# Attention and gated feed-forward on one core: head 0's bias rows built in place, V's first piece issued sooner, and the prologue's transposes and scores in another order

## The chip, the cores and the metric

One core of one Trainium2 chip. The metric is the device time of one execution in microseconds (us); before the change the median of 11 runs is 376.83 us (375.98 to 380.3). Engines are named as in the profile: PE is TensorE (PEld its weight loads), DVE is VectorE, ACT is ScalarE, POOL is GpSimd, SP is SyncE, which here only issues DMAs.

## The reference

Eight batches, eight heads, 576 positions, head size 64. Each head attends causally with a decay bias that comes from a running sum of `max(s, 0)`; the result, as 4608 rows of 512, goes through a gated feed-forward with 1536 hidden columns.

```python
scores = scale * np.matmul(q, k.transpose(0, 1, 3, 2))
cum = np.cumsum(np.maximum(s, 0.0), axis=-1)
bias = -(cum[:, :, :, None] - cum[:, :, None, :])
scores = np.where(causal, -1000000000.0, scores + np.minimum(bias, 0.0))
attn = np.exp(scores - np.max(scores, axis=-1, keepdims=True))
attn = attn / (np.sum(attn, axis=-1, keepdims=True) + 1e-09)
attn_out = np.matmul(attn, v)
# x: attn_out as (B * S, H * D)
g = x @ w_gate
out = (g * (1.0 / (1.0 + np.exp(-g))) * (x @ w_val)) @ w_out
```

## The kernel before, in words

**Bias as matrix rows.** A score is a product over 128 partitions. For an even row r of heads, 64 partitions hold q or k; the other 64 hold four bias rows and zeros. The running sum, scaled by 8 (`c8`), is split into a bf16 high part and a bf16 remainder. Two of the four rows multiply these parts on k's side by ones on q's side, the other two multiply q's parts by minus ones on k's side. All rows of all 64 heads stand in `HL` (partition = head, then four rows, then the q side and the k side). `aug` (L178) copies them by DMA, one head at a time, into `KQ[hb % 2][r]`, where `hb` is a group of four heads. A head is `hh` in its group, `r, e = divmod(hh, 2)`: r picks the tile, e its half of the columns. So heads 0 and 1 share `KQ[0][0]`, heads 2 and 3 share `KQ[0][1]`, heads 4 to 7 the two tiles of `KQ[1]`.

**The prologue.** SP loads s, then k and q of hb 0 in halves (row r = 0, then row 1). ACT, DVE and POOL fill the constant and zero parts of the tiles (L197 to L224; `pads` and `init_vt` are memsets on POOL). POOL then issues k's and q's loads of hb 1. DVE makes `HL` in a chain (L226 to L232): scale s, scan, high part, remainder, copy. k and q are cast to bf16 (`cast_half` for hb 0, `cast_one` for whole groups), transposed by PE into PSUM banks (`row_half` L886 for hb 0, `half_batch` L892 for hb 1) and copied out into `KQ` by `pe_out` (L305), which runs as L314 on ACT and as L316 on DVE. `keep_warm` issues products of the identity that nothing reads.

**The order by hand.** From L906 on, the calls stand in the order in which each engine gets its instructions; every engine and every queue works in that order[...]. `scores(h)` is four calls of `score_piece` (L338): a mask product (L353) for the pieces on the diagonal, the score products (L359), one exponential on ACT (L369). `values` is the product with V (L396) and the division on DVE (L412, L413). V is loaded in five pieces by POOL (`load_v` L151) and cast into `VT` by `cast_v` (L162), four pieces on POOL and one on DVE. `x_pe` transposes the attention's output, and `begin` (L630) starts the feed-forward. From then on `attn_items` and `ffn_items` are interleaved.

**Banks.** PSUM has eight banks. `take()` (L120) gives the one that was released longest ago, so the order of the calls also decides which earlier reader a product waits for. hb 1's transposed k and q hold four banks until their eight outputs are copied.

Of the kernel before, what the change touches and what calls it, by code (L numbers as in the profile page):

```python
# [12 lines left out]
FP32 = mybir.dt.float32  # L13
BF16 = mybir.dt.bfloat16
AF = mybir.ActivationFunctionType
ALU = mybir.AluOpType
# [3 lines left out]
def kernel(  # L20
# [11 lines left out]
    nc = tc.nc  # L32
    PSUM = bass.MemoryType.PSUM

    B, H, S, D = q.shape
# [42 lines left out]
    )  # L78

    NPE = 5  # L80
    XB = 2
    KS = {i: dram.tile([NR * S, 128], BF16, name=f"ks{i}") for i in range(NPE, NHB)}
    XS = {
# [11 lines left out]
    VT = [const.tile([128, NCH, H, D + 1], BF16, name=f"vt{i}") for i in range(2)]  # L95
    ident = const.tile([128, 128], BF16)
    one_s = const.tile([128, 1], FP32)
    HL = const.tile([BH, 4, 2, S], BF16)
    XR = 3 * TT
    XT = const.tile([128, 4, XR], BF16)  # L100
    warm = const.tile([128, 1], FP32)
    WS = const.tile([128, NFT // 2, 3, DM // 2], BF16)
    first_sbuf = ExitStack()
    first = first_sbuf.enter_context(tc.tile_pool(name="first", bufs=1))
    s_sb = first.tile([BH, S], FP32)
    c8 = first.tile([BH, S], FP32)
    PTP = {0: first, "bufs": 7}
    lower = first.tile([128, 512], BF16)

    with tc.manual_schedule():  # L110
# [76 lines left out]

        nc.sync.dma_start(s_sb, s.rearrange("b h n -> (b h) n"))
        def init_vt(i):
            nc.gpsimd.memset(VT[i][:, :, :, D : D + 1], 1.0)  # L190
            nc.gpsimd.memset(VT[i][64:128, 4, :, 0:D], 0.0)

        for r in range(NR):
            load_one(0, "k", (r, r + 1))
# [5 lines left out]
        nc.vector.memset(HL[:, 0:2, 0, :].bitcast(FP32), ONES2)  # L200
        nc.vector.memset(HL[:, 2:4, 1, :].bitcast(FP32), NEGS2)
        make_identity(nc, ident)
        nc.gpsimd.memset(lower, 0.0)
        nc.gpsimd.affine_select(
# [1 line left out]
            compare_op=ALU.is_ge, fill=nc.gpsimd.to_reg(MASKED), base=0, channel_multiplier=-1,  # L206
        )

        def pads(i):
            for r in range(2):  # L210
                nc.gpsimd.memset(KQ[i][r][64 * r : 64 * r + 64, :, NR * S :], 0.0)
# [8 lines left out]
        nc.vector.memset(aug_rows(1, 0), 0.0)  # L220
        for nm in ("k", "q"):
            load_one(1, nm, eng=nc.gpsimd)
        init_vt(0)
        pads(1)  # L224

        nc.vector.tensor_scalar(s_sb, s_sb, 0.0, 8.0, ALU.max, ALU.mult)  # L226
        nc.vector.tensor_tensor_scan(
            c8, one_s[0:BH, 0:1].to_broadcast([BH, S]), s_sb, 0.0, ALU.mult, ALU.add
        )
        nc.vector.tensor_copy(HL[:, 0, 1, :], c8)  # L230
        nc.vector.tensor_sub(HL[:, 1, 1, :], c8, HL[:, 0, 1, :])
        nc.vector.tensor_copy(HL[:, 2:4, 0, :], HL[:, 0:2, 1, :])  # L232

        SP4 = [nc.sync] * 4
        GP4 = [nc.gpsimd] * 4
# [69 lines left out]
        def pe_out(hb, name, g, r, eng):  # L305
            j0, j1 = JG[g]
            kq = SRC[name][1]
            dst = KQ[hb % 2][r][64 * r : 64 * r + 64, kq, 0 : NR * S].rearrange(
                "a (x j) -> a x j", j=J
            )[:, :, j0:j1]  # L310
            tp = tps[name, g]
            srcp = tp[0][64 * r : 64 * r + 64].rearrange("a j x -> a x j")
            if eng is nc.scalar:
                nc.scalar.copy(dst, srcp)  # L314
            else:
                eng.tensor_copy(dst, srcp)  # L316
            tp[2] -= 1
            if tp[2] == 0:
                give(tp[1])
# [577 lines left out]
        def scores(h):  # L897
            for ci in range(4):
                score_piece(h, ci)
# [23 lines left out]
        cast_one(1, "q", nc.vector)  # L923
        for c in range(3):
# [141 lines left out]
```

## Time and profile before

| | before |
|---|---|
| median of 11 runs | 376.83 us (375.98 to 380.3) |
| the profiled execution, its own time | 376.11 us |
| its span, first to last instruction | 374.4 us |
| mean granted TensorE clock | 0.998 |
| head 0's first score product | 11.02 us |
| first exponential | 11.45 us |
| first feed-forward product (L630) | 26.27 us |

The span is the time between the first and the last instruction of the profiled execution; the rest of its time lies around it. A row of the trace names start and duration in us, engine, line, operation, output and input with shapes, the number of instructions that were merged, and in square brackets the idle time before them with what ended it. All durations below come from this one execution. Busy times of TensorE are modelled and overlap, so one looks at the starts of its products.

### The profile page before, as it was taken

Reading aid. Unit: us, or ns where it says so; the run is one execution under the profiler, and the core shown is the slowest. Engines: PE = TensorE matmul, PEld = TensorE weight load, DVE = VectorE, ACT = ScalarE, POOL = GpSimd, SP = SyncE. Lnnn points to the kernel's source line nnn. Section 1 sums busy time; section 2 is a strip of 40 time slices with the busy share of each in tenths; the row PEclk is TensorE's granted clock in tenths of the full one; section 3 lists DMA queues with packets and bytes.
Section 4 is the critical chain, followed back from the end, with each engine's and each line's share of the span. In section 5 each row is a group of like instructions: output and inputs, shape, how many; then the busy total and the mean of one; then the engine's idle time right before and its main releaser. Section 6 shows DMA issues by size and latency. Waiting matters only on the chain.

```text
span 374.4 us, 8759 instructions
## 1 busy us (share of the span) xinstructions
PE 362.1 (97%) x3259; PEld 231.0 (62%) x3300; DVE 289.9 (77%) x578; ACT 240.3 (64%) x471; POOL 212.3 (57%) x325
## 2 busy tenths in 40 slices
PE   7799999999999999999999999999999999999995
PEld 6575556555555556855685559655865585476464
DVE  8968776468984899589967997699858867975984
ACT  8877776688876878588757875686566523323321
POOL 8983655856465647494649564955675516315320
PEclk9999999999999999999999999999999999999999
DMA  7899999899599997796769674995142103002003
GB/s 243 192 269 261 213 273 260 215 340 208 173 175 274 264 259 205 178 290 204 204 160 265 181 176 160 259 193 134 40 119 62 35 20 127 2 0 94 21 0 114
DMA packets 97146, 64.23 MB, mean 172 GB/s; under 512 B 77232, under 2 KB 82736, under 8 KB 97104
## 3 DMA queue, kind: packets, MB, share of 16 engines
q1 hardware_dynamic: 84976, 41.46, 46.3%
q0 software_dynamic: 12128, 22.21, 22.8%
q8 instruction: 26, 0.43, 0.5%
q14 instruction: 16, 0.13, 0.1%
HBM read 37.90 MB, written 19.86 MB: 154 GB/s over the span
## 4 chain that ended last, share of the span: by engine, by line
PE 90%; DVE 3%; ACT 3%; issue 1%; DMA 1%; POOL 1%; SPq 0%; DVEq 0%; ACTq 0%
PE bank L630 46%; PE bank L736 17%; PE bank L359 11%; PE bank L396 8%; PE bank L687 5%; ACT pt L369 2%; DVE kq L316 1%; DMA rawq<-in_q_dram 1%; PE bank L446 1%; ACT kq L314 1%; DVE pp L653 1%; POOL vt L168 1%; DVE ht L664 1%; PE bank L353 1%; PE bank L287 1%
## 5 line engine op out<-in xcount | busy, mean ns | idle before, releaser
L369 ACT ACTIVATE pt<-bank 128x512 bf16<-128x512 f32 (+1 forms) x256 | 120.3, 510 | 30.6 <-PE bank L359 17.3
L630 PE MATMUL bank<-XT,wg 128*128 128x512 bf16 x418 | 110.4, 379 | 1.3 <-DVE pp L653 0.3
L630 PE MATMUL bank<-XT,wv 128*128 128x512 bf16 x412 | 109.3, 379 | 1.1
L651 ACT ACTIVATE th<-bank 128x512 bf16<-128x512 f32 x108 | 64.7, 599 | 55.9 <-PE bank L630 50.2
L653 DVE SCALAR_TENSOR_TENSOR pp<-th,bank 128x512 bf16<-128x512 bf16 x108 | 73.7, 682 | 18.9 <-ACT th L651 18.4
L664 DVE SCALAR_TENSOR_TENSOR ht<-pp,bank 128x512 bf16<-128x512 bf16 x108 | 74.1, 686 | 10.6 <-PE bank L630 0.4
L359 PE MATMUL bank<-kq 128*128 128x128 bf16 (+4 forms) x576 | 75.8, 240 | 1.3 <-DMA kq<-HL 0.9
L673 POOL TENSOR_TENSOR ht<-ht 128x512 bf16<-128x512 bf16 x35 | 40.4, 1154 | 52.3 <-DVE su L671 52.2
L359 PEld LDWEIGHTS <-kq 128*128 128x128 bf16 x576 | 45.8, 98 | 31.5 <-issue 2.1
L630 PEld LDWEIGHTS <-wv 128*128 128x128 bf16 x432 | 38.4, 98 | 36.4 <-issue 0.6
L630 PEld LDWEIGHTS <-wg 128*128 128x128 bf16 x432 | 38.3, 98 | 34.3 <-issue 0.8
L374 POOL TENSOR_SCALAR_AFFINE_SELECT pt<-pt 128x512 bf16<-128x512 bf16 x56 | 36.8, 657 | 29.6 <-ACT pt L369 24.1
L396 PEld LDWEIGHTS <-pt 128*128 128x128 bf16 x960 | 41.7, 98 | 17.5 <-issue 0.3
L396 PE MATMUL bank<-vt,pt 128*128 128x65 bf16 x960 | 46.9, 194 | 0.3 <-POOL vt L168 0.3
L430 POOL DMA_DIRECT2D xs<-ot x24 | 21.7, 904 | 30.0 <-DVE ot L413 27.6
L736 PEld LDWEIGHTS <-ht 128*128 128x128 bf16 x336 | 31.2, 98 | 4.3
L413 DVE TENSOR_TENSOR ot<-bank,rc 128x320 bf16<-128x320 f32 x64 | 31.5, 491 | 2.2
L183 POOL DMA_DIRECT2D kq<-HL x48 | 28.9, 605 | 0.0
L736 PEld LDWEIGHTS <-su 128*128 128x128 bf16 x252 | 23.6, 98 | 3.3
L687 PE MATMUL bank<-wo,ht 128*128 128x512 bf16 x90 | 24.8, 379 | 0.3
L801 POOL TENSOR_TENSOR ysb<-ysb 128x512 f32<-128x512 f32 x12 | 15.2, 1270 | 15.3 <-DVE ysb L795 15.3
L379 POOL TENSOR_SCALAR_AFFINE_SELECT pt<-pt 128x64 bf16<-128x64 bf16 x56 | 14.8, 264 | 16.0 <-ACT pt L369 15.9
(93 smaller groups left out, 385.7 us busy)
## 6 DMA issues: line engine op xcount, KB each, us to landing
out_dram<-ysb POOLq DMA_DIRECT2D x32, 256.0 KB, 4.0
rawv<-in_v_dram SPq DMA_DIRECT2D x28, 256.0 KB
rawk<-in_k_dram SPq DMA_DIRECT2D x12, 576.0 KB
rawq<-in_q_dram SPq DMA_DIRECT2D x12, 576.0 KB
xs<-ot POOLq DMA_DIRECT2D x24, 160.0 KB, 3.6
ks<-ck SPq DMA_DIRECT2D x11, 288.0 KB
qs<-cq SPq DMA_DIRECT2D x11, 288.0 KB
rawk<-in_k_dram POOLq DMA_DIRECT2D x3, 576.0 KB, 7.0
```

The source lines that it names most:

```text
L359: nc.tensor.matmul(sc[:, o : o + w], T[:, 1, e * S + 128 * tj : e * S + 128 * (tj + 1)], T[:, 0, e * S + lo : e * S + hi], start=not maske ...
L369: nc.scalar.activation(pt[:, c0 : c0 + n], sc, AF.Exp, scale=0.125)
L374: nc.gpsimd.affine_select(pt[:, 1088:1600], pt[:, 1088:1600], pattern=[[0, 4], [1, 128]], compare_op=ALU.is_ge, fill=zreg, base=0, channel ...
L396: nc.tensor.matmul(av[:, bi * (D + 1) : (bi + 1) * (D + 1)], pt[:, c0 : c0 + 128], VT[b % 2][:, tj, h, :], start=(tj == 0), stop=(tj == bi),)
L413: nc.vector.tensor_mul(ot[:, :, e * D : (e + 1) * D], av3[:, :, 0:D], rc[:, :, None].to_broadcast([128, NCH, D]),)
L630: nc.tensor.matmul(view(bs, TT), w[:, c, f0 : f0 + 128], xt[:, c, :], start=(c == 0), stop=(c == 3),)
L651: nc.scalar.activation(th, pg, AF.Tanh, scale=0.5)
L653: nc.vector.scalar_tensor_tensor(pp, in0=th, scalar=1.0, in1=pg, op0=ALU.add, op1=ALU.mult)
L664: nc.vector.scalar_tensor_tensor(hp[:, 2 * k2 : 2 * k2 + 2, :].rearrange("p a n -> p (a n)"), in0=pp, scalar=0.5, in1=pv, op0=ALU.mult, op ...
L673: (nc.vector if ft == NFT - 1 else nc.gpsimd).tensor_sub(hp[:, 1:3, :], hp[:, 1:4:2, :], hp[:, 0:3:2, :])
L687: nc.tensor.matmul(view(pys[ts_], DM), hps[ft // 2][:, 2 * (ft % 2) + half, c0 : c0 + 128], WO[j][:, ft % WKO, :], start=(ft == 0), stop=( ...
L736: nc.tensor.matmul(ps, lhs(p), rhs(p), start=(first and p == 0), stop=(last and p == NP - 1), skip_group_check=True,)
```

## The change

- s's row of head 0 is loaded a second time, to two more partitions (64 and 65) of `s_sb`, by a DMA that ACT issues first of all. `s_sb`, `c8` and `HL` grow to 66 partitions.
- The remainder is now `HL_high * less + c8` with a scalar per partition: -1 for the 64 heads and for partition 65, 0 for partition 64. So the extra partitions hold the whole of `c8` in bf16 and the remainder, one under the other. Two copies of two partitions put them into `KQ[0][0]`, one on POOL (k's side, partitions 64 and 65), one on DVE (q's side, partitions 96 and 97); memsets put the ones and minus ones opposite. The DMA of head 0 in `aug(0)` is left out. Before hb 2 uses the tile, a memset on POOL clears rows 96 and 97.
- `pads(1)` and `init_vt(0)` go from POOL to DVE, ahead of the chain of s. The zero fill of `KQ[0][1]`'s first plane goes from ACT (L215) to POOL.
- V's first piece is issued before POOL's copy and cast; the other four ahead of the memset of `KQ[1][1]`.
- `keep_warm(10)` becomes 4, and the second one is left out. k's second row goes out half on ACT, half on DVE. Head 0's first three pieces stand ahead of q's row-1 transposes, the fourth behind; `half_batch` stands in the middle of head 2 and behind it; `values(0, 1)` stands behind `scores(6)`.

```diff
+    LR = 66
-    HL = const.tile([BH, 4, 2, S], BF16)
+    HL = const.tile([LR, 4, 2, S], BF16)
...
+    less = first.tile([LR, 1], FP32)
...
                 bh = hb * HB + hh
+                if bh == 0:
+                    continue
...
-        nc.sync.dma_start(s_sb, s.rearrange("b h n -> (b h) n"))
+        nc.sync.dma_start(s_sb[0:BH, :], s.rearrange("b h n -> (b h) n"))
+        nc.scalar.dma_start(s_sb[BH:LR, :], s[0, 0:1, :].to_broadcast([LR - BH, S]))
...
+        nc.vector.memset(less, -1.0)
+        nc.vector.memset(less[BH : BH + 1, :], 0.0)
...
         for r in range(2):
             nc.gpsimd.memset(aug_rows(0, r)[:, 1, :], 0.0)
-            nc.scalar.mul(
-                KQ[0][r][64 * (1 - r) : 64 * (1 - r) + 64, 0, :],
-                one_s[0:64, 0:1].to_broadcast([64, NR * S + 64]), 0.0,
-            )
+            if r == 0:
+                nc.scalar.mul(
+                    KQ[0][0][64:128, 0, :], one_s[0:64, 0:1].to_broadcast([64, NR * S + 64]), 0.0
+                )
+                nc.gpsimd.memset(KQ[0][0][96:98, 1, 0:S].bitcast(FP32), NEGS2)
         pads(0)
+        nc.gpsimd.memset(KQ[0][0][64:66, 0, 0:S].bitcast(FP32), ONES2)
+        nc.gpsimd.memset(aug_rows(0, 1)[:, 0, :], 0.0)
         nc.vector.memset(aug_rows(1, 0), 0.0)
         for nm in ("k", "q"):
             load_one(1, nm, eng=nc.gpsimd)
-        init_vt(0)
-        pads(1)
+        pads(1, nc.vector)
+        init_vt(0, nc.vector)
+        load_v(0, (0,), nc.gpsimd)
...
-        nc.vector.tensor_sub(HL[:, 1, 1, :], c8, HL[:, 0, 1, :])
-        nc.vector.tensor_copy(HL[:, 2:4, 0, :], HL[:, 0:2, 1, :])
+        nc.vector.scalar_tensor_tensor(
+            HL[:, 1, 1, :], in0=HL[:, 0, 1, :], scalar=less, in1=c8,
+            op0=ALU.mult, op1=ALU.add,
+        )
+        nc.gpsimd.tensor_copy(KQ[0][0][64:66, 1, 0:S], HL[BH:LR, 1, 1, :])
+        nc.vector.tensor_copy(KQ[0][0][96:98, 0, 0:S], HL[BH:LR, 1, 1, :])
+        nc.vector.tensor_copy(HL[0:BH, 2:4, 0, :], HL[0:BH, 0:2, 1, :])
...
-        def row_half(nm, r, eng):
+        def row_half(nm, r, eng, eng1=None):
             for g in range(2):
                 pe_transpose_half(0, nm, g, r)
             for g in range(2):
-                pe_out(0, nm, g, r, eng)
+                pe_out(0, nm, g, r, (eng, eng1 or eng)[g])
...
         cast_half(0, "q", 1, nc.gpsimd)
+        load_v(0, range(1, 5), nc.gpsimd)
         nc.gpsimd.memset(aug_rows(1, 1), 0.0)
-        load_v(0, range(5), nc.gpsimd)
         w_load("g", 0)
         aug(1, SP4)
-        keep_warm(10)
-        row_half("k", 1, nc.scalar)
+        keep_warm(4)
+        row_half("k", 1, nc.scalar, nc.vector)
+        for ci in range(3):
+            score_piece(0, ci)
         row_half("q", 1, nc.vector)
-        keep_warm(10)
+        score_piece(0, 3)
         cast_one(1, "k", nc.vector)
         cast_one(1, "q", nc.vector)
...
-        scores(0)
+        scores(1)
+        for ci in (0, 1):
+            score_piece(2, ci)
         half_batch("k")
-        scores(1)
+        for ci in (2, 3):
+            score_piece(2, ci)
         half_batch("q")
-        scores(2)
         scores(3)
...
         cast_v(0, 4, nc.vector)
+        nc.gpsimd.memset(KQ[0][0][96:98, 0, 0:S].bitcast(FP32), 0.0)
...
         scores(5)
+        scores(6)
         values(0, 1)
-        scores(6)
         values(2, 3)
```

More of the change, by code (lines that the diff above doesn't have):

```diff
@@ L104 @@
     first = first_sbuf.enter_context(tc.tile_pool(name="first", bufs=1))
-    s_sb = first.tile([BH, S], FP32)
-    c8 = first.tile([BH, S], FP32)
+    s_sb = first.tile([LR, S], FP32)
+    c8 = first.tile([LR, S], FP32)
+    less = first.tile([LR, 1], FP32)
     PTP = {0: first, "bufs": 7}
@@ L186, in aug, with init_vt @@
                 )
-        nc.sync.dma_start(s_sb, s.rearrange("b h n -> (b h) n"))
-        def init_vt(i):
-            nc.gpsimd.memset(VT[i][:, :, :, D : D + 1], 1.0)
-            nc.gpsimd.memset(VT[i][64:128, 4, :, 0:D], 0.0)
+        nc.sync.dma_start(s_sb[0:BH, :], s.rearrange("b h n -> (b h) n"))
+        nc.scalar.dma_start(s_sb[BH:LR, :], s[0, 0:1, :].to_broadcast([LR - BH, S]))
+        def init_vt(i, eng=nc.gpsimd):
+            eng.memset(VT[i][:, :, :, D : D + 1], 1.0)
+            eng.memset(VT[i][64:128, 4, :, 0:D], 0.0)
         for r in range(NR):
@@ L199 @@
         nc.scalar.activation(warm, warm, AF.Exp)
-        nc.vector.memset(HL[:, 0:2, 0, :].bitcast(FP32), ONES2)
-        nc.vector.memset(HL[:, 2:4, 1, :].bitcast(FP32), NEGS2)
+        nc.vector.memset(HL[0:BH, 0:2, 0, :].bitcast(FP32), ONES2)
+        nc.vector.memset(HL[0:BH, 2:4, 1, :].bitcast(FP32), NEGS2)
+        nc.vector.memset(less, -1.0)
+        nc.vector.memset(less[BH : BH + 1, :], 0.0)
         make_identity(nc, ident)
@@ L207, with pads @@
         )
-        def pads(i):
+        def pads(i, eng=nc.gpsimd):
             for r in range(2):
-                nc.gpsimd.memset(KQ[i][r][64 * r : 64 * r + 64, :, NR * S :], 0.0)
+                eng.memset(KQ[i][r][64 * r : 64 * r + 64, :, NR * S :], 0.0)
         for r in range(2):
             nc.gpsimd.memset(aug_rows(0, r)[:, 1, :], 0.0)
-            nc.scalar.mul(
-                KQ[0][r][64 * (1 - r) : 64 * (1 - r) + 64, 0, :],
-                one_s[0:64, 0:1].to_broadcast([64, NR * S + 64]), 0.0,
-            )
+            if r == 0:
[3 more added lines that the diff above has]
+                nc.gpsimd.memset(KQ[0][0][96:98, 1, 0:S].bitcast(FP32), NEGS2)
         pads(0)
+        nc.gpsimd.memset(KQ[0][0][64:66, 0, 0:S].bitcast(FP32), ONES2)
+        nc.gpsimd.memset(aug_rows(0, 1)[:, 0, :], 0.0)
         nc.vector.memset(aug_rows(1, 0), 0.0)
@@ L222 @@
             load_one(1, nm, eng=nc.gpsimd)
-        init_vt(0)
-        pads(1)
+        pads(1, nc.vector)
+        init_vt(0, nc.vector)
+        load_v(0, (0,), nc.gpsimd)
         nc.vector.tensor_scalar(s_sb, s_sb, 0.0, 8.0, ALU.max, ALU.mult)
         nc.vector.tensor_tensor_scan(
-            c8, one_s[0:BH, 0:1].to_broadcast([BH, S]), s_sb, 0.0, ALU.mult, ALU.add
+            c8, one_s[0:LR, 0:1].to_broadcast([LR, S]), s_sb, 0.0, ALU.mult, ALU.add
         )
         nc.vector.tensor_copy(HL[:, 0, 1, :], c8)
-        nc.vector.tensor_sub(HL[:, 1, 1, :], c8, HL[:, 0, 1, :])
-        nc.vector.tensor_copy(HL[:, 2:4, 0, :], HL[:, 0:2, 1, :])
+        nc.vector.scalar_tensor_tensor(
[5 more added lines that the diff above has]
+        nc.vector.tensor_copy(HL[0:BH, 2:4, 0, :], HL[0:BH, 0:2, 1, :])
         SP4 = [nc.sync] * 4
```

## The prediction

> **What bounds the kernel now.** I read the page's shares and its chain of work first, then a table by stretch of time, then the first 27 us in order of time, because the diff touches nothing later.
>
> ```profile
> PE 362.1 (97%) x3259; PEld 231.0 (62%) x3300; DVE 289.9 (77%) x578; ACT 240.3 (64%) x471; POOL 212.3 (57%) x325
> ...
> PE 90%; DVE 3%; ACT 3%; issue 1%; DMA 1%; POOL 1%; SPq 0%; DVEq 0%; ACTq 0%
> ```
>
> TensorE is busy 97% of the span and owns 90% of the chain that ended last: from the first feed-forward product on, a microsecond lost is a microsecond later at the end. The stretches (columns: width, then busy us of PE, PEld, DVE, ACT, POOL, granted clock, DMA share, GB/s) show where that is not so:
>
> ```profile
> 5.00:10.00 5.00, 3.99 (x56) 3.30 (x57) 4.82 (x8) 4.17 (x7) 4.75 (x9) 1.00 0.94 327
> 10.00:12.00 2.00, 1.14 (x18) 0.90 (x17) 1.97 (x3) 0.55 (x2) 2.00 (x3) 1.00 0.49 122
> 12.00:14.00 2.00, 1.95 (x28) 1.53 (x26) 1.97 (x4) 2.00 (x7) 2.00 (x3) 1.00 0.73 200
> 14.00:16.00 2.00, 1.43 (x14) 0.85 (x12) 1.97 (x3) 1.92 (x6) 2.00 (x4) 1.00 0.88 230
> 16.00:18.00 2.00, 1.53 (x14) 0.91 (x14) 2.00 (x4) 1.92 (x5) 1.40 (x3) 1.00 1.02 174
> 18.00:20.00 2.00, 2.00 (x34) 1.61 (x33) 0.67 (x2) 1.92 (x7) 2.00 (x4) 1.00 1.15 201
> 20.00:25.00 5.00, 5.00 (x113) 4.24 (x110) 3.35 (x11) 4.91 (x13) 3.60 (x6) 1.00 1.11 326
> ```
>
> To 18 us VectorE (DVE) has no gap: 4.82 of 5, then 1.97 to 2.00 of 2 four times running. From 12 us ScalarE's exponentials are full as well, and from 18 us TensorE is. So a gain in this prologue has to pass VectorE's queue. In order of time (start us, duration, engine):
>
> ```profile
> 2.50 1.07 DVE L220 MEMSET kq<- 64x1216 f32 x1 [0.29 <-issue]
> 3.80 0.52 DVE L226 TENSOR_SCALAR s_sb<-s_sb 64x576 f32<-64x576 f32 x1 [0.23 <-DMA s_sb<-in_s_dram]
> 7.17 0.53 DVE L232 COPY HL<-HL 64x1152 bf16<-64x1152 bf16 x1
> 7.62 2.96 DVE L316 COPY kq<-bank 64x640 bf16<-64x640 bf16 x4
> 10.62 0.76 DVE L246 CAST ck<-rawk 128x1152 bf16<-128x1152 f32 x1
> 11.02 0.83 PE L359 MATMUL bank<-kq 128*128 128x128 bf16 x8 [0.86 <-DMA kq<-HL]
> 11.45 13.52 ACT L369 ACTIVATE pt<-bank 128x512 bf16<-128x512 f32 x32 [1.56 <-PE bank L359]
> 12.45 5.65 DVE L316 COPY kq<-bank 64x640 bf16<-64x640 bf16 x8
> 19.63 1.08 PE L396 MATMUL bank<-vt,pt 128*128 128x65 bf16 x30
> 26.27 0.59 PE L630 MATMUL bank<-XT,wg 128*128 128x512 bf16 x2
> ```
>
> Head 0's first score product waits 0.86 us for the DMA that brings its bias rows, and the 32 exponentials of batch 0 then run almost without a gap. The feed-forward starts at 26.27.
>
> **Step 1, what comes ahead of s on VectorE.** The pads of hb 1 (two memsets of 64 elements as issued) and the fill of V's tile (40 and 512 elements) move from POOL to VectorE, ahead of L226. The memsets of 576 and 1216 elements took 0.538 and 1.072 us: 0.834 ns an element and 0.058 fixed. So 2 x 0.11 + 0.09 + 0.48 = 0.79, and 0.07 between neighbours (L200 ended 1.595, L201 began 1.664) five times is 0.35. L226 can then start at 3.57 + 0.79 + 0.35 = 4.7, not at 3.80. The 0.23 us wait for s vanishes in it; the two small memsets of `less` (0.06 each) fit the 0.29 us of issue ahead of L220. Cost 0.9 us; low end 0.6 with no spacing. The new load of two rows of s lands well before 4.7 (s's 64 rows, 32 times the bytes, landed by 3.8); its issue on ScalarE is bounded by SP's own issues, 0.42 to 0.59, and is paid for by the removed 1.2 us L215.
>
> **Step 2, the bias in place.** `tensor_sub` becomes a scalar_tensor_tensor on 66 partitions: same 576 columns, taken at the same 0.75. Two new copies of two partitions follow. VectorE's lies between half of L232 and all of it, 0.27 to 0.53; I take 0.3, it has half the columns. POOL's is near its 128x576 cast, 0.66. Hence the outputs of q's row 0 start at 7.62 + 0.9 + 0.3 = 8.8 and end 1.43 later (7.62 to 9.06 now), at 10.25. They, not the DMA, then release head 0: 10.3 against 11.02, first exponential near 10.75 against 11.45. **Gain so far: 0.7 us**, with the full 0.86 as its most while q's outputs are on time.
>
> POOL's copy must be there by 10.3. Ahead of it POOL gets two memsets of 288 columns (about 0.3 each, from 608 at 0.60 and 1216 at 1.10), one of 608 replaces ScalarE's L215, then batch-0's k and q loads (0.91, 0.74) and V's first piece (0.92): 4.42 + 1.2 = 5.6, + 2.6 = 8.2, copy done by 8.9, cast of q's row 1 by 9.6. [...] V's second issue, beside VectorE's casts, took 1.39 us where the first took 0.92. By the row POOL's copy ends at 9.4[...]. The moved-out 1.2 us also shifts k's and q's loads of hb 1 (landed 9.72 and 11.13, so about 11 and 12.4); their casts come later still.
>
> **Step 3, VectorE's debt.** After q's row 0, VectorE now has one more output (0.71, k's second group, taken from ScalarE), to 10.95. TensorE meanwhile does head 0's pieces 0 to 2 (0.65 us from first to last start) and only then q's row-1 transposes (0.69), so q's outputs start about 11.6: VectorE idles 0.6. They end at 13.05, where the casts of hb 1 started at 10.62 before. **2.4 us late.** The casts (1.8) and the eight outputs (5.65) follow: they end at about 20.5, not 18.10. The first four allow head 4: 17.7, when head 4 would be due with a 0.7 us lead (18.36 before). The last four each free one PSUM bank that head 5 needs, at 18.5, 19.2, 19.9 and 20.5. Head 5's last large piece thus gets its bank at 20.5 and its exponential starts about 20.95; before it was 20.86. The lead is gone.
>
> **Step 4, TensorE has nothing to put in.** values(0, 1) stood ahead of scores(6) and ran at 19.63; now it stands behind. TensorE, in order, waits at head 5's banks. Before, it was past head 5's last piece at 19.6 and needed 6.67 us to L630, with 0.3 of small waits. After, it passes at 20.9 with the same work: two pairs of values 1.9, scores(6) and (7) 1.9, then the 2.74 from 23.53 to 26.27: L630 at 27.4. **Net: 1.1 us later.** Low end 0.4 (step 1 at 0.6, small waits gone, steps overlapping), high end 1.8 (copy 0.53, `less` not hidden).
>
> V's first piece sooner, the other pieces about where they were, and the later 1.1 us memset of KQ[1][1] (heads 6 and 7 need it near 21) cost nothing: V's last cast ended at 19.2 and values start after 21.5. If values were not delayed, V sooner would be worth at most its 0.5 us wait at L168. Of the exchange of half_batch and head 2's pieces only the casts' lateness is used. The memset of rows 96 to 98 (0.3) stands behind 23 us on POOL, ahead of hb 2's casts, which had 1.4 us of slack (idle before L246).
>
> Removing 16 of the warm-up products costs nothing in work. [...] Before, 128-column products started 107 ns apart until 4.2 us and 56 ns apart ever after, across a gap of 0.86. [...]
>
> **Sum.** Span 374.4 + 1.1 = 375.5; the profiled execution 376.11 + 1.1 = 377.2; the median stands 0.72 above it, 376.83 + 1.1 = **377.9**. That is 0.3% slower, inside the 0.5% that a measurement of this kernel can about tell from no change.
>
> **Rivals.** A, the lead survives: if VectorE's early memsets cost little and its outputs finish by 18.5 or so, head 5 doesn't wait and the 0.7 us stays: 376.1. For it: ScalarE is full from 12 us. Against: VectorE's queue has no gap to catch up in. B, the clock halves after 8 us: [...] 3.3 in all: 380.1, slower beyond 0.5%. [...] C, the change doesn't do what it says: POOL's copy comes after 10.3 and head 0 waits for it as it did for the DMA; each us past 10.3 costs one, 0.7 makes head 0 no earlier: 378.6. D, q's load of hb 1 lands after 13.8, where VectorE wants to cast it, instead of 12.4; from there on one for one; with 1 us, 378.9.
>
> **Chances.** Forecast 0.62 (377.2 to 378.6), A 0.2 (375.9 to 377.2), B 0.06, C 0.06, D 0.06. The range 375.9 to 379.2 holds the forecast, A and most of C and D. Faster than 374.95 would need more than head 0's whole wait: 0.03. Slower than 378.7: B, half of C and D, and the forecast's upper tail, 0.14. Within: 0.83.
>
> **What would show it.** Right: L226 near 4.7; head 0's first product near 10.3 with no DMA behind its wait; hb 1's casts near 13; TensorE waiting for kq outputs (L316's line) between 17.5 and 20.9; first L630 near 27.4; the rest shifted alike. Wrong: L226 before 4.2, outputs done by 18.5, or a wait after 30 us on an engine that takes the shift up.

## The result and the profile after

The changed kernel took 379.68 us (median of 12 runs, 378.77 to 381.15) where the kernel before took 376.73 (47 runs): ratio 1.0074, 95% interval 1.0054 to 1.0094. It is slower by 2.95 us, where 1.1 was forecast, and lies above the forecast's range of 375.9 to 379.2 us. The profiled execution took 379.21 us with a span of 377.3, 2.9 more than before.

Of the page after, the same two lines as before, then the stretches (width, busy us of PE, PEld, DVE, ACT, POOL, granted clock, DMA share, GB/s):

```profile
PE 363.9 (96%) x3244; PEld 231.8 (61%) x3284; DVE 293.4 (78%) x586; ACT 238.9 (63%) x469; POOL 213.4 (57%) x326
...
PE 89%; DVE 6%; issue 2%; ACT 1%; POOL 1%; DMA 1%; DVEq 0%; ACTq 0%
```

```profile
5.00:10.00 5.00, 3.42 (x33) 2.74 (x33) 4.76 (x7) 3.40 (x6) 4.89 (x7) 1.00 0.75 262
10.00:12.00 2.00, 1.19 (x8) 0.72 (x7) 1.48 (x3) 0.57 (x2) 2.00 (x3) 0.60 1.06 331
12.00:14.00 2.00, 2.00 (x17) 1.38 (x16) 1.05 (x2) 1.23 (x4) 2.00 (x3) 0.54 0.97 235
14.00:16.00 2.00, 1.84 (x26) 1.31 (x24) 1.97 (x3) 1.74 (x5) 2.00 (x3) 1.00 1.02 211
16.00:18.00 2.00, 1.85 (x25) 1.32 (x23) 1.97 (x3) 1.57 (x5) 2.00 (x4) 1.00 0.94 111
18.00:20.00 2.00, 1.34 (x12) 0.72 (x11) 1.97 (x4) 1.66 (x4) 2.00 (x4) 1.00 1.15 208
20.00:25.00 5.00, 4.17 (x73) 3.14 (x71) 3.52 (x7) 4.90 (x12) 4.78 (x7) 1.00 1.10 325
```

VectorE's share of the chain has doubled, from 3% to 6%. The clock column shows something new: 0.60 and 0.54 between 10 and 14 us. And VectorE, which had no gap before 18 us, has one of 1.44 us that lies across two stretches: it is busy 1.48 of 2 and 1.05 of 2. In order of time (start, duration, engine):

```profile
4.88 0.46 DVE L238 TENSOR_SCALAR s_sb<-s_sb 66x576 f32<-66x576 f32 x1
8.17 0.35 DVE L248 COPY kq<-HL 2x576 bf16<-2x576 bf16 x1
8.55 0.85 DVE L249 COPY HL<-HL 64x1152 bf16<-64x1152 bf16 x1
9.32 2.19 DVE L333 COPY kq<-bank 64x640 bf16<-64x640 bf16 x3
12.95 1.47 DVE L333 COPY kq<-bank 64x640 bf16<-64x640 bf16 x2 [1.44 <-PE bank L318]
14.45 0.76 DVE L263 CAST ck<-rawk 128x1152 bf16<-128x1152 f32 x1
15.13 1.63 DVE L263 CAST cq<-rawq 128x1152 bf16<-128x1152 f32 x1
16.79 5.63 DVE L333 COPY kq<-bank 64x640 bf16<-64x640 bf16 x8
```

```profile
8.43 0.66 POOL L247 COPY kq<-HL 2x576 bf16<-2x576 bf16 x1
11.43 1.57 ACT L386 ACTIVATE pt<-bank 128x512 bf16<-128x512 f32 x3 [2.14 <-PE bank L376]
```

```profile
10.81 1.44 PE L376 MATMUL bank<-kq 128*128 128x128 bf16 x8 [1.75 <-DVE kq L333]
12.17 1.17 PE L318 MATMUL bank<-ident,cq 128*64 128x128 bf16 x9
...
21.12 0.38 PE L370 MATMUL bank<-lower,ident 128*128 128x512 bf16 x1 [0.42 <-DVE kq L333]
...
29.19 0.59 PE L647 MATMUL bank<-XT,wg 128*128 128x512 bf16 x2
```

The eight outputs end at 22.42 instead of 18.10, TensorE waits for them at 21.12, and the first feed-forward product comes at 29.19 instead of 26.27. That is 2.92 later, the span's whole difference: everything behind is shifted alike. Head 0's eight large products took 1.44 us instead of 0.83, and the nine transposes of q's row 1 behind them 1.17, where 0.69 is their time at full clock (experiment 1). Head 0's first product came 0.2 us sooner than before, but its first exponential came at 11.43, no sooner than the 11.45 of before; with the clock up, in experiment 1, it came at 11.22.

### The profile page after: what moved, and what is told of

Same layout as the page of the kernel before. It is cut to its first block, busy times and chain, and to the rows that moved or that the text cites. A ratio compares the mean times of both kernels' runs of the same rounds, so it can differ in the third digit from the quotient of the medians.

```text
span 377.3 us, 8744 instructions
## 1 busy us (share of the span) xinstructions
PE 363.9 (96%) x3244; PEld 231.8 (61%) x3284; DVE 293.4 (78%) x586; ACT 238.9 (63%) x469; POOL 213.4 (57%) x326
## 4 chain that ended last, share of the span: by engine, by line
PE 89%; DVE 6%; issue 2%; ACT 1%; POOL 1%; DMA 1%; DVEq 0%; ACTq 0%
PE bank L647 46%; PE bank L753 17%; PE bank L376 11%; PE bank L413 8%; PE bank L704 5%; DVE kq L333 3%; PE bank L463 1%; DMA s_sb<-in_s_dram 1%; PE bank L304 1%; DVE pp L670 1%; POOL vt L170 1%; DVE ht L681 1%; ACT pt L386 1%; DVE cq L263 0%; ACT kq L331 0%
## 5 line engine op out<-in xcount | busy, mean ns | idle before, releaser
L376 PE MATMUL bank<-kq 128*128 128x128 bf16 (+4 forms) x576 | 76.9, 242 | 3.0 <-DVE kq L333 2.3
```

The lines of the kernel that those rows point to most:

```text
L376: nc.tensor.matmul(sc[:, o : o + w], T[:, 1, e * S + 128 * tj : e * S + 128 * (tj + 1)], T[:, 0, e * S + lo : e * S + hi], start=not maske ...
```

## The experiments

Two theories to begin with. **Queue:** VectorE's debt is larger than forecast, because what was moved ahead of s and the work beside POOL cost more. **Clock:** a window of half clock, which the removed warm products would have prevented, costs the difference. Line numbers below shift by a few from kernel to kernel. Where a median and a trace disagree, the start of the first feed-forward product is the cleaner measure: behind it, a single execution may pick up half a microsecond or more at some later place, which has nothing to do with the prologue. Each kernel is compared with runs of the kernel before in its own group, whose medians were 376.56 to 376.85 us.

**1. Warm products alone (a_warm).**

```diff
-        keep_warm(4)
+        keep_warm(10)
         row_half("k", 1, nc.scalar, nc.vector)
+        keep_warm(20)
```

> The changed kernel with the warm-up products put back: 10 for 4 in front of k's row-1 transposes, and 20 more behind them, where TensorE waits anyway. Theory 1 (TensorE's clock was halved from 10.4 to 13.8 us because the warm-up products were taken out, and that costs about a microsecond): granted clock 1.0 from 8 to 16 us, q's row-1 outputs on VectorE start near 12.1 instead of 12.95, first feed-forward product near 28.3 instead of 29.16, time 0.8 to 0.9 us below the changed kernel, about 378.8. Theory 2 (VectorE's queue alone carries the loss): the clock comes back and the time stays within 0.3 us of 379.7.

Measured: 378.81 us, ratio 1.0060 (1.0047 to 1.0073). The clock stayed at 1.00 in the profiled execution, and 0.87 us went. So the clock, taken alone, was less than a third of the loss. The runs of the changed kernel agree. Each run has a mean clock on record, which doesn't say when the clock fell, but 3.41 us at half clock lower it by 0.0045; half clock behind the last products lowers it only to 0.997 in the traces (c2). Eight of the changed kernel's twelve runs have 0.995 or less, with a median of 379.70 us; of the four with 0.997 or more, three took 378.77 to 379.27 us, the fourth 381.15. In the trace the feed-forward began at 28.90, only 0.3 sooner, and its rows show why:

```profile
12.05 1.47 DVE L333 COPY kq<-bank 64x640 bf16<-64x640 bf16 x2 [0.55 <-PE bank L318]
13.56 1.37 DVE L263 CAST ck<-rawk 128x1152 bf16<-128x1152 f32 x1
14.85 1.62 DVE L263 CAST cq<-rawq 128x1152 bf16<-128x1152 f32 x1
16.50 5.63 DVE L333 COPY kq<-bank 64x640 bf16<-64x640 bf16 x8
```

```profile
11.55 0.69 PE L318 MATMUL bank<-ident,cq 128*64 128x128 bf16 x9
12.17 0.20 PE L370 MATMUL bank<-lower,ident 128*128 128x64 bf16 x1
12.95 0.20 PE L376 MATMUL bank<-kq 128*128 128x64 bf16 x1 [0.57 <-DMA kq<-HL]
```

VectorE waits 0.55 instead of 1.44 us, and the casts start 0.9 sooner. But now k's cast falls beside POOL's memset (13.18 to 14.31) and the issue behind it and takes 1.37 instead of 0.76, so 0.6 of the 0.9 is given back. A wait is also uncovered: head 0's last piece waits for a DMA of bias rows, though head 0 has its own in place. Its keys are columns 512 to 639 of a tile in which head 0 ends at 576; the last 64 are head 1's.

**2. POOL kept still while VectorE casts (a_hold, a_coldhold).** POOL's memset goes ahead of V's loads, and a small copy that reads VectorE's last cast holds back all that stands behind it on POOL. On top of the warm products, or alone (a_coldhold):

```diff
-        load_v(0, range(1, 5), nc.gpsimd)
         nc.gpsimd.memset(aug_rows(1, 1), 0.0)
-        w_load("g", 0)
+        load_v(0, range(1, 4), nc.gpsimd)
...
         cast_one(1, "q", nc.vector)
+        nc.gpsimd.tensor_copy(held, cts["q", 1][:, :, 0, 0])
+        load_v(0, (4,), nc.gpsimd)
+        w_load("g", 0)
```

> The changed kernel with the 26 warm products, and with POOL kept still while VectorE casts k and q of head block 1: the memset of KQ[1][1] goes ahead of V's second piece, and a small POOL copy that reads VectorE's last cast stands ahead of V's fifth piece, the gate weights' issue and V's casts. With the warm products alone the two casts took 1.37 and 1.62 us (0.76 for the shortest one anywhere) while POOL set memory, issued a load and cast V. Theory that POOL's work beside them lengthens them: 0.76 each, the eight outputs behind them end at 20.7 instead of 22.13, the first feed-forward product at 27.5 to 27.9 instead of 28.9, the time 377.4 to 377.8 against 378.81 us. Rival (the casts wait for their loads, or VectorE is as slow on a quiet POOL): casts of 1.3 us and more, time 378.6 or more, since V's casts come later.

Measured: 377.86 us, ratio 1.0034 (1.0020 to 1.0047). VectorE's rows, the row of POOL that was made to wait, and the first feed-forward product of TensorE:

```profile
13.56 0.76 DVE L264 CAST ck<-rawk 128x1152 bf16<-128x1152 f32 x1
14.23 0.75 DVE L264 CAST cq<-rawq 128x1152 bf16<-128x1152 f32 x1
15.02 5.63 DVE L334 COPY kq<-bank 64x640 bf16<-64x640 bf16 x8
```

```profile
15.05 0.20 POOL L944 COPY held<-cq 128x9 bf16<-128x9 bf16 x1 [1.50 <-DVE cq L264]
```

```profile
27.42 0.59 PE L648 MATMUL bank<-XT,wg 128*128 128x512 bf16 x2
```

The casts start at the same 13.56 as in experiment 1 and take 0.76 and 0.75 instead of 1.37 and 1.62. POOL's work beside them had made up the difference. The feed-forward starts 1.48 us sooner.

> The changed kernel with POOL kept still while VectorE casts head block 1, and nothing else: the warm products stay away. It fills the fourth corner beside after (379.68 us), warm products alone (378.81) and both (377.86). Theory that clock and POOL's work beside the casts are two separate terms of one queue: VectorE's wait for q's row-1 outputs stays near 1.4 us, the casts fall to 0.76 each, the eight outputs end near 21.6, the first feed-forward product near 28.3, the time 378.7 to 379.0 us. Rival (they are one and the same, quieting POOL gives all): near 377.9. Rival (the clock hides it): 379.5 or more.

Measured: 379.29 us, ratio 1.0069 (1.0050 to 1.0089). The trace has what the first theory asked for: a wait of 1.45 us, casts of 0.76 and 0.75, outputs ending at 21.55, the feed-forward at 28.32. The median is 0.3 above the expected band: the profiled execution lost 1.4 us more behind the prologue than that of the changed kernel, about 1 us of it in three waits near 250 us, and the runs spread from 378.05 to 380.43. So this median decides little; the rows show that clock and POOL are two terms of one queue. They are not separate: from 29.19 (neither), 28.90 (warm products), 28.32 (POOL still) and 27.42 (both) it follows that the warm products bring the feed-forward 0.29 us forward beside a busy POOL and 0.90 beside a still one.

**3. The memsets ahead of s (a_mem, a_warm_mem).** `pads(1)` and `init_vt(0)` back on POOL, behind the gate weights' issue, without and with the warm products.

```diff
-        pads(1, nc.vector)
-        init_vt(0, nc.vector)
...
         w_load("g", 0)
+        pads(1)
+        init_vt(0)
```

> The changed kernel with hb 1's pads and V's fill back on POOL, behind the first weight load. Theory 2 (VectorE's queue): the chain of s starts near 3.85 instead of 4.88, head 0's first product near 10.0 instead of 10.8, first feed-forward product near 27.9 instead of 29.16, time 1.0 to 1.3 us below the changed kernel, about 378.5. Theory 1 (clock alone): TensorE idles less, but with as few warm-up products the clock halves again; then the time moves by less than 0.4 us.

> The changed kernel with the 26 warm products and with the four small memsets of pads(1) and init_vt(0) back on POOL, behind the issue of the gate weights. With the warm products alone it took 378.81 us, and there VectorE took up s at 4.88 us. Queue theory (what stands ahead of s on VectorE costs its time): s at 3.8, q's row-0 outputs start at 8.4 instead of 9.32, the casts of head block 1 at 12.7 instead of 13.56, the first feed-forward product 0.9 us sooner: 377.9 us, granted clock 1.0 throughout. Rival (the lost time sits behind the prologue's casts, and an earlier start is used up in waiting there): q's outputs start sooner, but the casts end as late as before and the time stays at 378.6 to 378.9.

Measured: 378.20 (1.0039, 1.0024 to 1.0053) and 378.51 us (1.0057, 1.0040 to 1.0073). With the warm products s is taken up at 3.78, q's outputs start at 8.58, the casts at 12.81, and the feed-forward at 27.86, 1.04 sooner than in experiment 1. In the median only 0.30 of that shows, within the spread of its six runs (377.99 to 379.82), so the 377.9 of the theory was missed. The profiled execution of a_mem, taken without warm products, shows a longer stretch of half clock. It took 381.51 us, while its other five runs, with a mean clock of 0.997 or more, took 377.98 to 378.56:

```profile
10.00:12.00 2.00, 1.94 (x14) 1.30 (x14) 0.73 (x2) 1.32 (x3) 2.00 (x3) 0.52 0.87 303
12.00:14.00 2.00, 0.76 (x7) 0.46 (x5) 1.76 (x3) 0.25 (x1) 2.00 (x3) 0.50 1.00 248
14.00:16.00 2.00, 1.16 (x7) 0.76 (x8) 1.77 (x2) 0.26 (x2) 1.95 (x4) 0.50 0.99 208
16.00:18.00 2.00, 2.00 (x14) 1.28 (x13) 0.00 (x0) 1.88 (x5) 1.82 (x5) 0.50 0.95 135
18.00:20.00 2.00, 2.00 (x21) 1.88 (x20) 1.19 (x2) 1.27 (x3) 2.00 (x4) 0.50 1.14 207
```

Half clock lasted 10.2 us here. In TensorE's rows head 0's last piece, at 14.84, waits 2.08 us for head 1's bias rows, and VectorE stands still for 3.04 us until the transposes behind it come. So clock and DMA together made these 3 us, and this trace doesn't part them.

**4. The order of TensorE and the warm products in the kernel before (a_qfirst, b_cold).** a_qfirst puts `row_half("q", 1)` ahead of all four pieces of head 0. b_cold is the kernel before with `keep_warm(4)` and without the second call.

> The changed kernel with q's row-1 transposes back in front of head 0's pieces. Theory 2: VectorE's wait of 1.44 us in front of q's row-1 outputs shrinks to 0.2 or less, hb 1's casts start near 13.2 instead of 14.45, time 0.8 to 0.9 us below the changed kernel, about 378.8, although the clock may still halve. Rival (the order of transposes and scores is harmless, since TensorE waits there anyway): within 0.3 us of 379.7.

> The kernel before with only the warm-up products thinned as the change does: 4 for 10, and the second 10 left out. Theory 1: the granted clock falls to 0.5 for one window of 3.4 us somewhere between 7 and 15 us, and the time rises by 0.8 to 1.3 us, to about 377.8. Theory 2: TensorE's transposes and the gap of 1 us are enough work for the clock; granted clock 1.0, time within 0.3 us of 376.75.

Measured: a_qfirst 378.24 us (1.0050, 1.0035 to 1.0065), the feed-forward at 28.89; a window of half clock lay at 7.52 to 10.93, ahead of head 0. The median is 1.4 us below that of the changed kernel, more than expected; the trace, one of the slower of the six runs (378.76), is only 0.3 sooner. VectorE's wait is gone and its casts start at 12.88, but:

```profile
12.88 2.04 DVE L263 CAST ck<-rawk 128x1152 bf16<-128x1152 f32 x1
```

Beside the same memset and issue of POOL, k's cast ends at 14.92. In experiment 1 it began 0.7 us later and ended at 14.93; the eight outputs start at 16.50 in both. So here the earlier start of the casts is lost. It need not be: in a_warm_mem (experiment 3) k's cast began at 12.81 and took 0.95, and it was POOL's memset that took longer, 1.64 instead of 1.13. What decides which of the two gives way is open. Five of the six runs had a mean clock of 0.995 or less, and the sixth, at 1.000, took 378.17, hardly less than the best of the five (378.20). So in this order no price of the clock is seen, though one run at full clock is little to go by.

b_cold took 377.63 us (1.0022, 1.0007 to 1.0037), 376.12 to 380.13 in 20 runs. Its profiled execution stayed at full clock and began the feed-forward at 26.41, 0.14 later than before, so its trace doesn't show the clock's price. The mean clocks of the runs do: nine with 0.995 or less have a median of 377.97 us, eleven with 0.998 or more one of 376.53, no more than the kernel before. So with fewer warm products the clock falls in some runs and not in others, and in the old order a run in which it falls is 1.4 us longer. Of the kernel before, one to three of the 25 to 44 runs of each group had 0.995 or less.

**5. The other edits, one after the other (a_hold_val, a_wmkqv, a_inpl, a_inpl2, a_inpl3).** a_hold_val is a_hold with `values(0, 1)` ahead of `scores(6)`.

> The kernel with warm products and still POOL (377.86 us), and values(0, 1) ahead of scores(6) again. Theory that TensorE has nothing to put in while it waits for head 5's banks because these products stand behind scores(6): they fill waits of some 0.3 us, the first feed-forward product at 27.0 to 27.2 instead of 27.42, the time 377.5. Rival (V's last cast, which VectorE does behind its outputs at 20.7 to 21.3, holds them back anyway): no change, 377.8 to 377.9, or a little later since scores(6) waits behind them.

Measured: 377.23 us (1.0021, 1.0009 to 1.0033), but the feed-forward starts at 27.42 in both. So the place of these products costs nothing in the prologue. a_hold's profiled execution took 0.6 us more behind it, 0.4 of that in one wait near 135 us; why, and whether the medians differ by 0.63 us for the same reason, is open.

a_wmkqv takes a_warm_mem and undoes k's output on VectorE, the place of head 0's pieces, and the place of the values. a_inpl restores the order of heads 0 to 2 and `half_batch` as well. a_inpl2 has the warm products where the kernel before has them, and a_inpl3 also issues V's first piece with the others:

```diff
-        load_v(0, (0,), nc.gpsimd)
...
-        load_v(0, range(1, 5), nc.gpsimd)
+        load_v(0, range(5), nc.gpsimd)
```

> The changed kernel with everything undone but head 0's bias rows in place, V's first piece and the exchange of head 2's pieces with half_batch: warm products, the four memsets on POOL, k's second group out on ScalarE, q's row-1 transposes ahead of head 0's pieces, values(0, 1) ahead of scores(6). Theory that the time was lost in these five edits: within 0.2% of the kernel before, 376.6 to 377.3 us. Rival that the in-place bias itself is what costs (its two-partition copies, with POOL's beside VectorE's, in the queue that has no gap): at least 0.3% slower than before, 377.8 us or more.

> Head 0's bias rows in place and V's first piece sooner, with all the rest as in the kernel before: memsets on POOL, warm products, k's second group out on ScalarE, q's row 1 ahead of head 0, scores(0) and half_batch and scores(1) in the old order, values ahead of scores(6). The kernel that still had the new order of head 1, head 2 and half_batch took 378.10 us; there TensorE waited 1.44 us for the DMA of head 1's bias rows ahead of head 0's last piece, and head block 1's transposes stood behind that and head 1. Theory that this exchange is what held it: the eight outputs start at 13.9 to 14.1 instead of 15.27, the first feed-forward product at 26.3 to 26.9 instead of 27.67, the time 376.7 to 377.3. Rival (the in-place copies hold it): 377.9 or more.

> Head 0's bias rows in place and V's first piece sooner, all else in the old order, and now with the warm products where the kernel before has them (10 ahead of k's row-1 transposes, 10 behind q's), since 20 of them ahead of q's transposes delayed those. Theory that the in-place bias still leaves TensorE to wait for a DMA: head 0's last piece takes 128 columns of k of which 64 are head 1's, so it waits for head 1's bias rows (landing near 13.0, against 11.0 for head 0's in the kernel before); head block 1's transposes and head 1 stand behind it, ScalarE idles 0.5 to 1 us near 13, the eight outputs end near 19.6, the first feed-forward product at 26.9 to 27.4, the time 377.2 to 377.8 us. Rival (with everything else restored the bias in place is worth its 0.7 us): the first feed-forward product by 25.8, 376.3 or less.

> As the run with the bias in place and the old order and warm products, but V's first piece is issued with the other four, as in the kernel before: only the bias in place is left of the change. Theory that V's first piece sooner does harm (POOL's issue of 0.91 us stands ahead of the copy of head 0's rows and of the cast of q's row 1, and its 256 KB lie ahead of the bias rows of head 1): the cast of q's row 1 ends 0.9 us sooner, those rows land at 12 to 12.5 instead of 13, the time 0.3 to 0.6 us less than with it, 376.8 to 377.2 us. Rival (it is harmless, as predicted): the same time within 0.2 us.

Measured, with the start of the feed-forward in brackets: a_wmkqv 378.10 us (1.0041, 1.0025 to 1.0057) [27.67]; a_inpl 378.12 us (1.0044, 1.0028 to 1.0060) [29.35, in a window of half clock, with 20 warm products ahead of q's transposes]; a_inpl2 377.73 us (1.0044, 1.0012 to 1.0076) [27.51]; a_inpl3 377.06 us (1.0011, 0.9998 to 1.0023) [26.71]. The theories of a_wmkqv and a_inpl missed by 0.8 us each, and the new order of heads 1 and 2 is hardly the reason: a_inpl2, without it and with the warm products in their old place, starts the feed-forward only 0.16 sooner than a_wmkqv. In a_inpl2 a fallen clock is dear: three of its ten runs, with a mean clock of 0.994 or less, took 380.25 to 380.86 us, the other seven 377.55 to 378.73. a_inpl2 and a_inpl3, in TensorE's rows:

```profile
9.95 0.69 PE L316 MATMUL bank<-ident,cq 128*64 128x128 bf16 x9 [1.26 <-POOL cq L271]
...
12.91 0.20 PE L374 MATMUL bank<-kq 128*128 128x64 bf16 x1 [0.71 <-DMA kq<-HL]
```

```profile
11.71 0.19 PE L367 MATMUL bank<-lower,ident 128*128 128x64 bf16 x1
11.74 0.19 PE L373 MATMUL bank<-kq 128*128 128x64 bf16 x1
```

With V's first piece ahead, POOL's cast of q's row 1 comes later, and TensorE's transposes wait 1.26 us for it. Then head 0's last piece waits 0.71 us for head 1's rows. Without it, neither wait is there. What is left in a_inpl3, little more than the bias in place, makes no difference that shows in the median, and its feed-forward starts 0.44 us later than before.

**6. V's first piece in the changed order (a_warm_v0).** Experiment 1 with the edit of a_inpl3.

> The changed kernel with the warm products, and with V's first piece issued with the other four again. In the old order of TensorE's work this was worth 0.67 us in the median (377.73 to 377.06), through the cast of q's row 1 and the landing of head 1's bias rows. Theory that in the changed order VectorE's queue hides both: the cast isn't waited for, head 0's last piece is no longer held by the DMA (0.57 us with the warm products alone), but the casts of head block 1 and the outputs behind them stay where they are, 13.5 and 22.1; the time 378.6 to 378.9 against 378.81 us. Rival (the earlier issue costs the same 0.7 us here): 378.0 to 378.3.

Measured: 380.07 us (1.0086, 1.0057 to 1.0116), slower by 1.3 than experiment 1, where the theories allowed no change or a gain. The feed-forward starts at 29.95, 1.05 later than there. VectorE's rows:

```profile
8.17 0.79 DVE L247 COPY kq<-HL 2x576 bf16<-2x576 bf16 x1
8.99 0.84 DVE L248 COPY HL<-HL 64x1152 bf16<-64x1152 bf16 x1
...
14.22 1.21 DVE L262 CAST ck<-rawk 128x1152 bf16<-128x1152 f32 x1
15.35 2.17 DVE L262 CAST cq<-rawq 128x1152 bf16<-128x1152 f32 x1
```

POOL's copy now starts at 8.13, just ahead of VectorE's of the same size, which takes 0.79 instead of 0.35. And q's cast meets three of POOL's casts of V (15.72 to 17.99) and takes 2.17. Some 0.2 us of the 1.05 have another source: in this execution ten warm products from 8.36 took 1.21 us, in experiment 1 0.73, and VectorE waited 0.76 us for q's row 1 instead of 0.55. The same edit is worth minus 0.67 us in one order, through what waits for POOL, and plus 1.26 in the other, mostly through what it puts beside what.

**7. Can the earlier bias pay at all? (c2, c3, c5, c5v)** c2 keeps the bias in place and gives VectorE nothing for it. POOL does the small memsets late, and ScalarE copies q's two rows. There are ten and six warm products, and all of row 1 goes ahead of the scores:

```diff
-        nc.vector.tensor_copy(KQ[0][0][96:98, 0, 0:S], HL[BH:LR, 1, 1, :])
+        nc.scalar.copy(KQ[0][0][96:98, 0, 0:S], HL[BH:LR, 1, 1, :])
...
+        scores(0)
         scores(1)
-        for ci in (0, 1):
-            score_piece(2, ci)
         half_batch("k")
-        for ci in (2, 3):
-            score_piece(2, ci)
         half_batch("q")
+        scores(2)
         scores(3)
```

> A version meant to keep the gain of the in-place bias and nothing of its price: POOL fills V's tile, the pads and the constant bias rows late, ScalarE makes the copy of the two rows of k behind its last cast, k's second group goes out on ScalarE, ten and six warm products, both row-1 halves ahead of head 0's scores, scores(0) and scores(1) ahead of head block 1's transposes. If VectorE's debt was the whole loss: its outputs end within 0.4 us of the 18.10 of the kernel before, head 0's first exponential comes near 10.9 instead of 11.45, and the time is 376.0 to 376.8, no slower than before. Rival (the outputs' end, not the exponentials, sets the first feed-forward product even then): 377 us and more.

c3 adds the still POOL of a_hold and issues V on SP. c5 is c2 with `half_batch("q")` behind `scores(2)`. c5v is c5 with `values(0, 1)` ahead of `scores(6)`.

> The version with the bias rows in place but nothing of the price (377.14 us) with POOL kept still while VectorE casts head block 1, V's five pieces issued on SP behind the bias rows' loads, and the gate weights' issue, the pads and the fill of V's tile behind the casts. There the casts took 1.14 and 1.12 us and ScalarE waited 0.51 us ahead of head 2. Theory: casts of 0.76 each, no wait ahead of head 2, the outputs end near 18.5 instead of 19.17, the exponentials run without a gap from 10.9 to 24.5 and the first feed-forward product comes at 25.8 to 26.1 against 26.27 of the kernel before: 376.1 to 376.5 us. Rival (V's loads on SP come in the way of the bias rows or of head block 1's q): no gain on 377.1.

> The version with the bias rows in place but nothing of the price (377.14 us), with q's half of head block 1's transposes behind head 2 instead of ahead of it, since ScalarE stood idle 0.51 us while TensorE waited there for VectorE's cast of q. Theory: the exponentials of heads 1 and 2 follow each other, the last one of batch 0 ends near 24.7 instead of 25.23, VectorE's outputs end no later than 19.4, the first feed-forward product at 26.0 to 26.1 against 26.27 of the kernel before, the time 376.4 to 376.7 us. Rival (q's outputs come later and head 4 or 5 waits for them): 377 or more.

> The version with the bias rows in place, nothing of the price and head 2 ahead of q's half (377.23 us), with values(0, 1) ahead of scores(6) as in the kernel before. There the exponentials ran without a gap from 10.86 to 22.45 and then stood idle 1.04 us ahead of head 7, because TensorE did four heads of values first. Theory: with two of the four ahead of head 6 the gap goes, the last exponential of batch 0 ends near 24.3 to 24.6 instead of 25.19, the first feed-forward product at 25.8 to 26.0 against 26.27 of the kernel before, the time 376.1 to 376.6 us. Rival (V's casts, which end at 20.1, hold the values and with them head 6): 377 or more.

Measured: c2 377.14 us (1.0008, 0.9994 to 1.0022), feed-forward at 26.52; c5 377.23 us (1.0011, 1.0000 to 1.0022), 26.48; c5v 377.43 us (1.0019, 1.0004 to 1.0035), 26.31. The first exponential comes at 10.92, 10.86 and 10.84 instead of 11.45, so the gain of 0.6 us is there, but none of it reaches the feed-forward. ScalarE stands idle 0.51 us ahead of head 2 in c2, 1.05 ahead of head 7 in c5, and in c5v 0.58 ahead of head 6, whose place in TensorE's order is behind values that wait for POOL's cast of V's fourth piece (to 20.08). The theories, 376.0 to 376.8 us, all missed: no version here beats the kernel before.

c3 took 385.75 us (1.0243, 1.0219 to 1.0268). Its casts took 0.76 and 0.75, but V's five loads on SP went ahead of the bias rows of heads 4 to 7 in the same queue:

```profile
25.58 1.44 PE L373 MATMUL bank<-kq 128*128 128x128 bf16 x8 [7.91 <-DMA kq<-HL]
```

## Why the prediction was wrong, step by step

VectorE's queue decided, as forecast. The table shows when it reached each point (us); "warm", "still" and "both" are a_warm, a_coldhold and a_hold.

| | before | foreseen | after | warm | still | both |
|---|---|---|---|---|---|---|
| s taken up | 3.80 | 4.7 | 4.88 | 4.88 | 4.88 | 4.88 |
| q's row-0 outputs start | 7.62 | 8.8 | 9.32 | 9.32 | 9.32 | 9.32 |
| q's row-1 outputs start | 9.13 | 11.6 | 12.95 | 12.05 | 12.96 | 12.06 |
| casts start | 10.62 | 13.05 | 14.45 | 13.56 | 14.45 | 13.56 |
| eight outputs end | 18.10 | 20.5 | 22.42 | 22.13 | 21.55 | 20.65 |
| first feed-forward product | 26.27 | 27.4 | 29.19 | 28.90 | 28.32 | 27.42 |
| median of the runs | 376.73 | 377.9 | 379.68 | 378.81 | 379.29 | 377.86 |

**Step 4, from debt to time: right.** The forecast turned 2.4 us of debt into 1.1 us of time, so 1.3 was lead. Measured: 22.42 - 18.10 = 4.32 of debt, 2.92 of time, 1.40 of lead; the other three kernels of the table leave 1.40 as well. But its remark on the values behind `scores(6)` was idle: moving them back left the feed-forward at 27.42 (a_hold_val).

**Step 1: right in kind, 0.18 short.** s at 4.88 instead of 4.7; putting the memsets back gave 1.04 us at the feed-forward.

**Step 2: right that POOL's copy is in time (done at 9.09), wrong on what it does to VectorE.** q's row-0 outputs start 0.52 us late; 0.18 of that is step 1's, and most of the rest is lost here. The forecast asked only how much later POOL would be beside VectorE, not the other way round. POOL's two-row copy ran from 8.43 to 9.09, and VectorE's L249 beside it took 0.85, where L232, beside a memset of POOL, took 0.53. No run leaves POOL's copy out, so this cause is read from the overlap.

**Step 3: the size is wrong, by the clock and by POOL.** The wait for q's row 1 was foreseen as 0.6; it was 1.44 at half clock, and 0.55 with the clock up. The two casts were foreseen as 1.8 in all, from the 0.76 and 1.12 of before. From the first one's start to the last one's end they took 2.31, and 2.91 with the clock up, since they then met more of POOL's work; with POOL still, 1.42. Counting 0.52 for the later start, 0.88 from there to the casts, and 0.52 for the casts gives 1.92: the gap between 2.4 and 4.32.

**The step that failed** is step 3's debt: 2.4 us foreseen, 4.32 measured. Of the 1.92 between them the clock made 0.88, POOL's work beside VectorE 0.52 in the casts and some 0.3 in step 2, and step 1 made 0.18. The clock's share was put at nothing. That was the author's estimate: the trace of before had shown products 56 ns apart across a gap of 0.86 us, but not what longer gaps do. Rival B was given 0.06, and its clock did halve, from 10.41 to 13.82. But its price of 2.2 us (3.3 in all, less the forecast's 1.1), an estimate too, was too high in its turn: it was 0.87 in the median and 0.3 in the trace, because the casts that started sooner took longer beside POOL (experiment 1), and 0.90 in the trace with POOL still (experiment 2). POOL's share is the second miss: that VectorE's casts take longer beside its work (1.37 and 1.62 us in a_warm, 0.76 and 0.75 in a_hold) has no rival in the forecast, which took the casts' 1.8 over from before. With both taken away the changed kernel takes 377.86 us and starts the feed-forward at 27.42, where the forecast said 377.9 and 27.4. The agreement is partly luck: the later start of 0.5 us is still in it, and casts shorter than foreseen by 0.4 make up for it.

**Rivals A, C and D** did not occur: no lead was left even at the first exponential (11.43), POOL's copy was done 1.7 us before head 0's first product (10.81), and q's cast followed k's with no wait for its load.

One thing no step had: building head 0's rows in place doesn't free TensorE from the DMA of bias rows. Head 0's last piece reads 64 columns of head 1, and head 1 follows anyway. In the changed kernel the slow clock hid this wait; with the clock up it was 0.57 us, in a_wmkqv 1.44.

## What to carry to other kernels

Work that is moved between VectorE and POOL has to be priced in pairs: ask what each long SBUF copy or cast will lie beside, on both engines, since the same edit gave 0.67 us in one order and cost 1.26 in another. Warm-up products did their work in the middle of this stage as well, where products are sparse, not only at the start: in b_cold, with fewer of them, nine of 20 runs had a mean clock of 0.995 or less and were 1.4 us longer. And when an input is built in place to avoid a transfer, look at the last reader's address range before counting the wait as gone.

## What the runs showed of the hardware

**Half clock came behind 3.41 us in which TensorE was busy 1.62.** The stretch ahead of the halved one in the kernel after, the halved one, and the one of the kernel before that holds the same work as the first (columns as in the stretches above):

```profile
7.00:10.41 3.41, 1.62 (x18) 1.06 (x17) 3.24 (x6) 1.74 (x3) 3.30 (x5) 1.00 0.87 292
10.41:13.82 3.41, 3.01 (x20) 1.94 (x20) 1.94 (x4) 1.74 (x4) 3.41 (x5) 0.50 1.00 269
```

```profile
7.69:11.10 3.41, 2.19 (x30) 1.81 (x32) 3.31 (x6) 1.65 (x3) 3.34 (x5) 1.00 0.71 276
```

In the kernel after, 128-column products started 107 ns apart in the halved stretch (head 0's from 10.87, q's transposes from 12.28) and 56 ns apart from 13.84 on, in unbroken rows of one shape. Up to 7.00 they had started 107 ns apart as well, and in the kernel before up to 4.2, though the clock column reads 1.00 there.

The clock column reads 0.50 for 3.41 us in a_qfirst (from 7.52), a_coldhold (from 10.36) and a_inpl (from 8.17) too, and in a_mem for three times as long (10.08 to 20.32). In the 3.41 us ahead of half clock TensorE was busy, by the profile, 1.00 us (c3, from 16.20), 1.48 (a_qfirst), 1.62 (after), 1.68 (a_coldhold), 1.69 (a_inpl) and 1.76 (a_mem). Stretches of the same length with 1.75 (b_cold, from 8.62), 1.90 (a_inpl3, from 4.63) and 1.97 us (a_wmkqv, from 11.49) were followed by full clock. So busy time as modelled doesn't part them: 1.75 us came ahead of full clock, 1.76 ahead of half. What does part them, no run here shows. In a_mem the first two 3.41 us at half clock, busy 2.68 and 2.07, were followed by half clock, the third, busy 3.41, by full clock; in the other four the halved stretch, busy 2.97 (a_coldhold) to 3.38 (a_inpl), was followed by full clock.
